# Product stage of a long convolution: sums by 64-row matmuls in two turns, another order of units, the weight additions earlier

## The chip, the cores and the metric

The kernel runs on one core of one Trainium2 chip. A core has a matmul engine (TensorE; the profile's PE, with PEld for its weight loads), VectorE (DVE), ScalarE (ACT), GpSimd (POOL), and SyncE (SP), which here only issues DMAs. They run side by side and wait for each other through semaphores. Matmuls write to PSUM, a memory of eight banks of 512 float32 per partition; all else lies in SBUF. The metric is device time in microseconds (us), lower is better.

## The reference

Two layers on 2048 tokens of width 512: a convolution as long as the sequence, gated by the layer-normed input, and a dense MLP with ReLU, both with a residual:

```python
def _A_ref(q, k, v, shift_k, ssm_k, ssm_D):      # q is layernorm(x)
    for t in range(ks):                          # ks = 4 taps
        k_shift = k_shift + k_pad[:, t:t + S, :] * shift_k[:, ks - 1 - t][None, None, :]
    kv = k_shift * v
    kv_f = rfft(kv padded to 2 S);  kf_f = rfft(ssm_k padded to 2 S)
    y = irfft(kv_f * kf_f)[:, :S, :]
    return q * (y + kv * ssm_D)

h = x + _A_ref(_layernorm(x), A_k, A_v, A_shift_k, A_ssm_k, A_ssm_D)
h2 = h + relu(_layernorm(h) @ w1) @ w2
```

(The transforms are shortened here: they stand in the original with their axes and reshapes.)

## The kernel before

The transforms are matmuls with sine tables, in two steps each. The kernel's stages, in order: taps and first step of the transforms (`pkv`, `ps`: lines 335 and 300), the **product stage** (lines 426 to 469), two steps back (`psi`, line 555; `pz`, line 646), and the MLP (`ps1m`, `ps2m`: lines 658 and 674). Each engine runs its instructions in the order in which the program gives them; nothing reorders them, so the loops below are the order.

When the product stage begins, `BK` holds the half-transformed convolution kernel and `BX` the half-transformed input, both 128 partitions by 2 by 32 by 64 values of kind float32r. For each of 32 indices `k1` the stage must finish the transform of both and multiply them. It does this in **units**. A unit takes a pair of PSUM banks (`bank2`, four such pairs in the pool `psF`) and fills it in two halves: columns 0 to 255 of both banks from `BK` (K half), columns 256 to 511 from `BX` (X half).

- `pairs(k1)`, tile `u`: the two halves of the partitions apart. For each of K and X, two steps `i` accumulate, and in each step two matmuls of 64 rows by 128 columns, one on partitions 0 to 63, the other on 64 to 127, go to the first and to the second bank. The weights are columns of the sine table `st`. There are 32 such units.
- `sums(k1)`, tile `us`: two indices `k1` and `k1 + 1` at once, one bank each, by matmuls of 128 rows by 128 columns, two accumulating steps each for K and X. The weights are `smc`, sums and differences of the sine table that POOL makes a chunk at a time (`sum_tables`, line 383), three chunks ahead, in three buffers. There are 16 such units.

`times(unit)` ends a unit: ScalarE copies its K half to SBUF (`ktu` or `kts`, two buffers each, line 423), and VectorE multiplies the X half in PSUM with that copy (line 450). The product of a `u` unit overwrites column `k1` of `BK`, that of a `us` unit two columns at the front of `BX`; after it, the bank pair is free for a later unit.

Eight chunks `c` of four indices each run in turn (line 454), each with the units u0 to u3 (`pairs(4c)` to `pairs(4c + 3)`), s0 and s1 (`sums(4c)`, `sums(4c + 2)`). TensorE's order in a chunk is u0, u1, s0, s1, u2, u3, each unit's K half and then its X half; in the first chunk the K halves of u0, u1, s0, s1 come ahead of their X halves. The products are taken in the order u0, u1, s0, s1, u2, u3.

POOL also adds up the four row blocks of the weight `w1` (`add_chunks`, line 416, three steps) into parts of `st` that are no longer wanted; TensorE makes column means of it right behind the stage (`column_means`, line 478, tile `pm`). In the program these steps stand behind the chunks 4, 5 and 6. `w1` itself is loaded on SP's queue at the start of the stage (line 408); the next load on that queue, of `x` (line 493), is issued when the stage is over.

Of the kernel before, what the change touches and what calls it, by code (L numbers as in the profile page):

```python
# [15 lines left out]
P = 128  # L16
# [40 lines left out]
def kernel(  # L57
# [13 lines left out]
    nc = tc.nc  # L71
# [9 lines left out]
    halves = (lo, hi)  # L81
# [15 lines left out]
    BK = bkp.tile([P, 2, 32, 32, DC * 2], F32R, tag="K", name="BK")  # L97
# [52 lines left out]
    def bank2(name):  # L150
        return psum.tile([P, 2, 512], F32, tag="ps", name=name)[:]
# [65 lines left out]
    st = stp.tile([P, 32, 192], F32R, name="st")  # L217
# [157 lines left out]
    smc = skp.tile([P, 3, 2, 4, P], F32R, name="smc")  # L375
# [3 lines left out]
    def sum_tables(c):  # L379
        ks = slice(4 * c, 4 * c + 4)  # L380
        for dp, pq in enumerate(halves):
            for i, op in ((0, ALU.subtract), (1, ALU.add)):
                nc.gpsimd.tensor_tensor(out=smc[pq, c % 3, i, :, 64 * dp:64 * dp + 64], in0=st[pq, ks, 64:128].bitcast(F32),  # L383
                                        in1=st[pq, ks, 0:64].bitcast(F32), op=op)
# [12 lines left out]
    BX = BXt[:, :, 2:66, :].rearrange("p g (i k) x -> p i g k x", i=2)  # L397
# [16 lines left out]
    def add_chunks(step):  # L414
        o, a, b = ((wsum, w1[:, 0, :], w1[:, 1, :]), (wpair, w1[:, 2, :], w1[:, 3, :]), (wsum, wsum.bitcast(F32), wpair.bitcast(F32)))[step]
        nc.gpsimd.tensor_tensor(out=o, in0=a, in1=b, op=ALU.add)

    def cols(B, pq, k1, i):
        return B[pq, i].rearrange("p (u w) (v s) x -> p u w v (s x)", w=2, s=2)[:, :, k1 % 2, k1 // 2, :]

    def forms(ps, tag):
        kt = prod.tile([P, 2, 256], F32, tag=tag, name=tag, bufs=2)
        nc.scalar.copy(out=kt[:], in_=ps)  # L423
        return kt

    def pairs(k1):

        ps = bank2("u")

        def do(x):  # L430
            for i, t in ((0, st[:, k1, 64:192]), (1, st[:, k1, 0:128])):
                for dp, pq in enumerate(halves):
                    nc.tensor.matmul(out=ps[:, dp, 256 * x:256 * x + 256], lhsT=t[pq], rhs=cols((BK, BX)[x], pq, k1, i),  # L433
                                     start=(i == 0), stop=(i == 1), tile_position=(64 * dp, 0), skip_group_check=True)
        return do, ps, "ktu", BK[:, :, :, k1, :]

    def sums(k1):
        ps = bank2("us")

        def do(x):  # L440
            for k in (k1, k1 + 1):
                for i in range(2):
                    nc.tensor.matmul(out=ps[:, k % 2, 256 * x:256 * x + 256], lhsT=smc[:, k // 4 % 3, i, k % 4, :],  # L443
                                     rhs=cols((BK, BX)[x], slice(0, P), k, i), start=(i == 0), stop=(i == 1), skip_group_check=True)
        return do, ps, "kts", BXs[:, :, k1:k1 + 2, :].rearrange("p g k x -> p k g x")

    def times(unit):
        do, ps, tag, o = unit
        kt = forms(ps[:, :, 0:256], tag)
        nc.vector.tensor_tensor(out=o, in0=ps[:, :, 256:512].rearrange("p b (g x) -> p b g x", x=8),  # L450
                                in1=kt[:].rearrange("p b (g x) -> p b g x", x=8), op=ALU.mult)


    for c in range(8):
        units = [pairs(4 * c), pairs(4 * c + 1), sums(4 * c), sums(4 * c + 2)]

        for n, x in sorted(((n, x) for n in range(4) for x in range(2)), key=lambda nx: nx[::-1] if c == 0 else nx):
            units[n][0](x)
        for k1 in (4 * c + 2, 4 * c + 3):
            times(units.pop(0))  # L460
            units.append(pairs(k1))
            for x in range(2):
                units[-1][0](x)
        for unit in units:
            times(unit)
        if c + 3 < 8:
            sum_tables(c + 3)
        if c in (4, 5, 6):
            add_chunks(c - 4)

    FS = 344
    cen = {}
# [25 lines left out]
    st = late.tile([P, 4, 6], F32, name="st")  # L498
# [260 lines left out]
```

## Time and profile before

| | |
|---|---|
| median of 3 runs | 208.73 us (208.56 to 209.94) |
| the profiled execution's own time | 208.83 us |
| its span on the core | 206.4 us |
| busy: TensorE, VectorE, ScalarE, POOL | 96%, 69%, 57%, 34% |
| product stage in that execution | 49.55 (first matmul of a unit) to 87.42 (end of the last product) |
| 64-row matmuls of `u`: 256 of them | 0.28 us each, two at a time |
| 128-row matmuls of `us`: 128 of them | 0.28 us each |
| copies on ScalarE: 48 | 0.59 us each |
| products on VectorE: 48 | 0.68 us each |
| granted TensorE clock over the span | 0.994 of full speed |

The span is the time from the first to the last instruction of the core; the execution's own time has 2.4 us more around it. Matmuls follow each other before the one ahead has ended, so a matmul's duration is longer than its share of the engine; the starts tell what one costs. In the timeline, a row merges equal instructions that follow each other: start, time from the first's start to the last's end, engine, line, operation, output and inputs, shapes, how many; then in brackets how long the engine had been idle ahead of it and which work ended that.

### The profile page before, as it was taken

The page shows a single profiled execution, that of the slowest core. Times are in us where ns is not written, and L with a number is a line of the kernel's source. Part 1 is how long each engine was busy: PE and PEld are TensorE (multiplying, and loading weights), DVE is VectorE, ACT ScalarE, POOL GpSimd, SP SyncE. Part 2 cuts the span into 40 slices and gives each one's busy share as a digit, 9 for nine tenths or more (in the row PEclk, how much of TensorE's full clock was granted, in tenths as well). Part 3 has the DMA queues.
Part 4 walks back from the last instruction along what each step waited for, and adds up shares of the span by engine and source line. Part 5 has one row for each costly group of instructions (what it writes and reads, how often), then busy time and mean ns, then how long its engine had stood idle before and what let it go on. Part 6 is the DMA issues. An engine that isn't in the chain of part 4 may idle for free.

```text
span 206.4 us, 4344 instructions
## 1 busy us (share of the span) xinstructions
PE 198.7 (96%) x1733; PEld 138.3 (67%) x1741; DVE 141.8 (69%) x246; ACT 117.3 (57%) x190; POOL 69.5 (34%) x118
## 2 busy tenths in 40 slices
PE   8999999998999999999999999999999999999991
PEld 2575556877899998899998944466444844444450
DVE  5989898698689989997743775899079742261131
ACT  5776789787687787777692068403950065026300
POOL 7963801991555699232003032042202010002000
PEclk9999999999999999999999999999999999999997
DMA  5999990001600000035515999999906717110011
GB/s 147 353 205 168 203 162 6 0 5 21 258 0 0 3 0 3 0 105 102 96 35 180 229 224 121 212 145 134 114 17 118 161 25 91 42 56 17 0 51 51
DMA packets 47818, 19.91 MB, mean 96 GB/s; under 512 B 42710, under 2 KB 46264, under 8 KB 47800
## 3 DMA queue, kind: packets, MB, share of 16 engines
q1 hardware_dynamic: 44144, 16.15, 42.4%
q10 hardware_dynamic: 3656, 3.51, 6.0%
q8 instruction: 13, 0.21, 0.4%
q14 instruction: 5, 0.04, 0.1%
HBM read 7.02 MB, written 2.10 MB: 44 GB/s over the span
## 4 chain that ended last, share of the span: by engine, by line
PE 94%; DVE 2%; ACT 1%; issue 1%; ACTq 0%
PE ps1m L658 18%; PE ps2m L674 18%; PE psi L555 11%; PE u L433 8%; PE us L443 8%; PE ps L300 8%; PE pz L646 7%; PE pkv L335 7%; PE psz L156 4%; PE pst L284 4%; DVE BK L450 1%; ACT ktu L423 1%; ACT BX L273 0%; DVE BK L312 0%; ACT BK L315 0%
## 5 line engine op out<-in xcount | busy, mean ns | idle before, releaser
L660 ACT ACTIVATE M<-ps1m 128x512 bf16<-128x512 f32 (+1 forms) x44 | 25.1, 595 | 49.4 <-PE ps1m L658 28.1
L674 PE MATMUL ps2m<-M 128*128 128x512 bf16 (+3 forms) x183 | 38.5, 366 | 0.2
L674 PEld LDWEIGHTS <-M 128*128 128x128 bf16 (+1 forms) x187 | 18.3, 98 | 19.9
L658 PEld LDWEIGHTS <-w 128*128 128x128 bf16 (+1 forms) x176 | 17.4, 100 | 19.9
L383 POOL TENSOR_TENSOR smc<-st 64x256 fp32r<-64x256 f32 x32 | 22.8, 731 | 13.6 <-PE us L443 12.8
L517 POOL TENSOR_SCALAR rstd<-mv 128x4 f32<-128x4 f32 x8 | 2.2, 277 | 70.1 <-DVE mv L515 70.1
L676 DVE SCALAR_TENSOR_TENSOR M<-ps2m,rstd,M 128x512 bf16<-128x512 f32 (+1 forms) x13 | 9.1, 705 | 22.6 <-PE ps2m L674 13.5
L450 DVE TENSOR_TENSOR BK<-u,ktu 128x512 fp32r<-128x512 f32 x32 | 20.6, 685 | 4.9 <-PE us L443 2.7
L555 PE MATMUL psi<-inv,BK 128*128 128x128 f32 x128 | 21.1, 255 | 0.0
L423 ACT COPY ktu<-u 128x512 f32<-128x512 f32 x32 | 18.0, 588 | 5.1 <-DVE BK L450 2.4
L555 PE MATMUL psi<-inv,BX 128*128 128x256 f32 x64 | 20.5, 338 | 0.1
L555 PEld LDWEIGHTS psi<-inv,BK 128*128 128x128 f32 x128 | 19.7, 197 | 0.0
L658 PE MATMUL ps1m<-M,w 128*128 128x512 bf16 (+1 forms) x88 | 19.3, 379 | 0.0
L658 PE MATMUL ps1m<-xT,w 128*128 128x512 bf16 (+1 forms) x88 | 19.3, 379 | 0.0
L433 PE MATMUL u<-BK,st 64*128 64x256 f32 x128 | 14.2, 303 | 0.0
L433 PE MATMUL u<-BX,st 64*128 64x256 f32 x128 | 13.0, 283 | 0.0
L555 PEld LDWEIGHTS psi<-inv,BX 128*128 128x128 f32 x64 | 12.1, 196 | 0.4 <-DVE BK L450 0.4
L513 DVE BATCH_NORM_STATS2 st<-M 128x6 f32<-128x512 bf16 x20 | 12.3, 677 | 0.0
L315 ACT CAST BK<-ps 128x512 fp32r<-128x512 f32 x16 | 9.3, 585 | 5.0 <-PE ps L300 3.4
L632 DVE TENSOR_TENSOR qT<-pz,qT 128x2048 bf16<-128x2048 f32 x2 | 4.6, 2291 | 10.7 <-DMA qT<-M 6.5
L443 PE MATMUL us<-BK,smc 128*128 128x256 f32 x64 | 10.8, 294 | 0.7 <-ACT BX L273 0.6
L450 DVE TENSOR_TENSOR BX<-us,kts 128x512 fp32r<-128x512 f32 x16 | 10.9, 685 | 0.8
(126 smaller groups left out, 405.5 us busy)
## 6 DMA issues: line engine op xcount, KB each, us to landing
E<-in_A_ssm_k_dram SPq DMA_DIRECT2D x1, 2048.0 KB
out_dram<-M ACTq DMA_DIRECT2D x15, 128.0 KB
w<-in_B_w_dram SPq DMA_DIRECT2D x1, 1376.0 KB
M<-in_B_w_dram ACTq DMA_DIRECT2D x1, 1280.0 KB
M<-in_A_q_dram SPq DMA_DIRECT2D x8, 128.0 KB
xh<-in_A_q_dram SPq DMA_DIRECT2D x4, 128.0 KB
xr<-in_A_q_dram SPq DMA_DIRECT2D x4, 128.0 KB
out_dram<-M ACTq DMA_DIRECT2D x2, 64.0 KB
```

What stands on the lines that cost most here:

```text
L300: nc.tensor.matmul(out=pss[rp][:, gi // 2, :, gi % 2, :], lhsT=fl[rows, 2 * g:2 * g + 2, :].rearrange("p d n -> p (d n)"), rhs=f[rows].rea ...
L335: nc.tensor.matmul(out=ps[:, i, :], lhsT=wdiag[:, r0 + i, j, :], rhs=kT[c][:, r0 + i, 16 - j:CH + 16 - j], start=(j == 0), stop=(j == KS - 1))
L383: nc.gpsimd.tensor_tensor(out=smc[pq, c % 3, i, :, 64 * dp:64 * dp + 64], in0=st[pq, ks, 64:128].bitcast(F32), in1=st[pq, ks, 0:64].bitcas ...
L423: nc.scalar.copy(out=kt[:], in_=ps)
L433: nc.tensor.matmul(out=ps[:, dp, 256 * x:256 * x + 256], lhsT=t[pq], rhs=cols((BK, BX)[x], pq, k1, i), start=(i == 0), stop=(i == 1), tile ...
L443: nc.tensor.matmul(out=ps[:, k % 2, 256 * x:256 * x + 256], lhsT=smc[:, k // 4 % 3, i, k % 4, :], rhs=cols((BK, BX)[x], slice(0, P), k, i) ...
L450: nc.vector.tensor_tensor(out=o, in0=ps[:, :, 256:512].rearrange("p b (g x) -> p b g x", x=8), in1=kt[:].rearrange("p b (g x) -> p b g x", ...
L555: nc.tensor.matmul(out=o if part == 0 else o[:, P * part - P:P * part], lhsT=src[:, g // 2, :, g % 2::2].rearrange("p c r -> p (c r)"), rh ...
L646: nc.tensor.matmul(out=pz[:, i, :, a:a + w, :].rearrange("p (s r) a n -> p s r (a n)", s=2), lhsT=ax[rho][:, n2 // 2, n2 % 2, :], rhs=ecor ...
L658: nc.tensor.matmul(out=ps1[:fsz, :].rearrange("p (i t) -> p i t", i=4), lhsT=w1[:, c, fc * P:fc * P + fsz], rhs=hT[sc][:, :, c, :], start= ...
L660: nc.scalar.activation(out=h1T[:fsz, fc, :], in_=ps1[:fsz, :], func=ACT.Relu)
L674: nc.tensor.matmul(out=ps2, lhsT=h1T[:ksz, fc, i * P:(i + 1) * P], rhs=w2[:ksz, fc, d0:d0 + w], start=(fc == 0), stop=(fc == NFC - 1))
```

## The change

The sums become matmuls of 64 rows too. A 128-row matmul of index `k` is now two matmuls, of partitions 0 to 63 and of 64 to 127, that add into the same bank. Each K or X half of a unit of sums is done in two **ways**: in way 1 the lower rows work on the first index (first bank) while the upper rows work on the second (second bank); in way 2 they are swapped. A no-operation of TensorE stands where the way changes and waits for the last matmuls of the other way, so that the two row halves never write to one bank at the same time. Only the first matmuls of a unit have the flag that starts a sum; all others add or, on columns not yet written, write.

The order of the units is written out as two strings, one for the first chunk and one for the others. `s0K1` is the K half of s0 in way 1, `u1X` the X half of u1, `=s0` the product of s0. The units of sums now alternate with the others, in three to five stretches each, and so the order of the products changes as well: u1, s0, u0, s1, u2, u3 in the first chunk, then u0, s0, u1, s1, u3, u2.

The three additions for `w1` move to behind the chunks 2, 4 and 5.

```diff
     def sums(k1):
+
         ps = bank2("us")
-
-        def do(x):
-            for k in (k1, k1 + 1):
-                for i in range(2):
-                    nc.tensor.matmul(out=ps[:, k % 2, 256 * x:256 * x + 256], lhsT=smc[:, k // 4 % 3, i, k % 4, :],
-                                     rhs=cols((BK, BX)[x], slice(0, P), k, i), start=(i == 0), stop=(i == 1), skip_group_check=True)
+        begun = []
+        ways = {}
+
+        def do(what):
+            x, way = "KX".index(what[0]), int(what[1])
+            last = {}
+            for i in range(2):
+                for dp, pq in enumerate(halves):
+                    k = k1 + (dp + way - 1) % 2
+                    if i == 0 and dp == 0 and (3 - way, dp) in ways:
+
+                        turn = nc.tensor.nop()
+                        for d in range(2):
+                            tc.add_manual_dep(turn.ins, ways[3 - way, d], mybir.DependencyInfo(mybir.DependencyClass.Sync, mybir.DependencyReason.DATA))
+                    mm = nc.tensor.matmul(out=ps[:, k % 2, 256 * x:256 * x + 256], lhsT=smc[pq, k // 4 % 3, i, k % 4, :],
+                                     rhs=cols((BK, BX)[x], pq, k, i), start=not begun, stop=(i == 1 and what in begun),
+                                     tile_position=(64 * dp, 0), skip_group_check=True)
+                    last[dp] = mm.ins.name
+                begun.extend((what[0] + "12"[2 - way], i))
+            for dp in range(2):
+                ways[way, dp] = last[dp]
         return do, ps, "kts", BXs[:, :, k1:k1 + 2, :].rearrange("p g k x -> p k g x")
...
+    FIRST = "s0K2 u1K s1K2 s0K1 u0K s1K1 s0X1 u1X =u1 s0X2 =s0 s1X1 u0X =u0 s1X2 =s1 u2K u2X u3K =u2 u3X =u3"
+    OTHER = "s0K1 s0X1 u0K u0X s0K2 u1K =u0 s0X2 =s0 s1K1 s1X1 u1X =u1 s1K2 s1X2 =s1 u3K u2K u3X =u3 u2X =u2"
     for c in range(8):
-        units = [pairs(4 * c), pairs(4 * c + 1), sums(4 * c), sums(4 * c + 2)]
-
-        for n, x in sorted(((n, x) for n in range(4) for x in range(2)), key=lambda nx: nx[::-1] if c == 0 else nx):
-            units[n][0](x)
-        for k1 in (4 * c + 2, 4 * c + 3):
-            times(units.pop(0))
-            units.append(pairs(k1))
-            for x in range(2):
-                units[-1][0](x)
-        for unit in units:
-            times(unit)
+        units = {}
+        for step in (OTHER if c else FIRST).split():
+            if step[0] == "=":
+                times(units[step[1:]])
+                continue
+            u = step[:2]
+            if u not in units:
+                units[u] = (pairs if u[0] == "u" else sums)(4 * c + (1 if u[0] == "u" else 2) * int(u[1]))
+            units[u][0](step[2:])
         if c + 3 < 8:
             sum_tables(c + 3)
-        if c in (4, 5, 6):
-            add_chunks(c - 4)
+        if c in (2, 4, 5):
+            add_chunks(max(c - 3, 0))
```

In `pairs` only the start flag changes in the same manner, and the halves are named K and X.

More of the change, by code (lines that the diff above doesn't have):

```diff
@@ L428, in pairs @@
         ps = bank2("u")
-        def do(x):
-            for i, t in ((0, st[:, k1, 64:192]), (1, st[:, k1, 0:128])):
+        begun = []
+        def do(what):
+            x = "KX".index(what[0])
+            for i in range(2):
+                t = st[:, k1, 64:192] if i == 0 else st[:, k1, 0:128]
                 for dp, pq in enumerate(halves):
                     nc.tensor.matmul(out=ps[:, dp, 256 * x:256 * x + 256], lhsT=t[pq], rhs=cols((BK, BX)[x], pq, k1, i),
-                                     start=(i == 0), stop=(i == 1), tile_position=(64 * dp, 0), skip_group_check=True)
+                                     start=not begun, stop=(i == 1), tile_position=(64 * dp, 0), skip_group_check=True)
+                begun.append(i)
         return do, ps, "ktu", BK[:, :, :, k1, :]
@@ L438, in sums, with do @@
         ps = bank2("us")
-        def do(x):
-            for k in (k1, k1 + 1):
-                for i in range(2):
-                    nc.tensor.matmul(out=ps[:, k % 2, 256 * x:256 * x + 256], lhsT=smc[:, k // 4 % 3, i, k % 4, :],
-                                     rhs=cols((BK, BX)[x], slice(0, P), k, i), start=(i == 0), stop=(i == 1), skip_group_check=True)
+        begun = []
+        ways = {}
+        def do(what):
+            x, way = "KX".index(what[0]), int(what[1])
+            last = {}
+            for i in range(2):
+                for dp, pq in enumerate(halves):
[11 more added lines that the diff above has]
+                ways[way, dp] = last[dp]
         return do, ps, "kts", BXs[:, :, k1:k1 + 2, :].rearrange("p g k x -> p k g x")
```

## The prediction

> **What bounds the kernel now.** I read the page first (engine shares, the chain), then the timeline of the product stage (49.6 to 87.4 us), the only stage that the change touches, and last the groups of its lines.
>
> ```profile
> PE 198.7 (96%) x1733; PEld 138.3 (67%) x1741; DVE 141.8 (69%) x246; ACT 117.3 (57%) x190; POOL 69.5 (34%) x118
> PE 94%; DVE 2%; ACT 1%; issue 1%; ACTq 0%
> ```
>
> TensorE ends nearly every wait, so a change there is worth what it takes from TensorE, as long as the next bound is far. In this stage it is not far. One chunk of the steady part:
>
> ```profile
> 77.33 0.41 PE L433 MATMUL u<-BX,st 64*128 64x256 f32 x4
> 77.43 1.29 DVE L450 TENSOR_TENSOR BK<-u,ktu 128x512 fp32r<-128x512 f32 x2
> ...
> 77.58 0.43 PE L433 MATMUL u<-BK,st 64*128 64x256 f32 x4
> ...
> 77.85 0.41 PE L433 MATMUL u<-BX,st 64*128 64x256 f32 x4
> 78.21 1.18 ACT L423 COPY ktu<-u 128x512 f32<-128x512 f32 x2 [0.33 <-DVE BK L450]
> 78.24 0.55 PEld L443 LDWEIGHTS us<-BK,smc 128*128 128x128 f32 x4 [0.20 <-issue]
> 78.27 0.73 PE L443 MATMUL us<-BK,smc 128*128 128x256 f32 x4
> 78.72 0.55 PEld L443 LDWEIGHTS us<-BX,smc 128*128 128x128 f32 x4
> 78.84 0.65 PE L443 MATMUL us<-BX,smc 128*128 128x256 f32 x4
> 79.11 1.29 DVE L450 TENSOR_TENSOR BK<-u,ktu 128x512 fp32r<-128x512 f32 x2 [0.39 <-PE us L443]
> ...
> 79.32 0.64 PE L443 MATMUL us<-BK,smc 128*128 128x256 f32 x4
> ...
> 79.80 0.64 PE L443 MATMUL us<-BX,smc 128*128 128x256 f32 x4
> ...
> 80.37 0.51 PE L433 MATMUL u<-BK,st 64*128 64x256 f32 x4
> ...
> 80.72 0.42 PE L433 MATMUL u<-BX,st 64*128 64x256 f32 x4
> ...
> 82.60 0.54 PEld L443 LDWEIGHTS us<-BK,smc 128*128 128x128 f32 x4 [0.21 <-issue]
> ```
>
> From start to start a group of four 64-row matmuls (two pairs, each pair side by side) takes 0.24 us, and four 128-row matmuls take 0.48. So a pair of 64 rows costs the same 0.1215 us as one matmul of 128 rows; call this a **slot**. A chunk has 32 slots, 3.89 us, but lasts 82.60 - 78.24 = 4.36. The missing 0.47 lies at the two crossings between the forms. Into the sums: 77.85 + 0.24 = 78.09 was due, it starts at 78.27, and its first four take 0.57 for 0.48: together 0.27. Out of them: 79.80 + 0.48 = 80.28 was due, it starts at 80.37, and its first four take 0.35 for 0.24: 0.20.
>
> VectorE sits close behind: two products take 1.29 us, each 0.685, so they follow each other every 0.605, and six per chunk want 3.63 of the 4.36; its idle 0.39 waits for the sums.
>
> **What sets when a bank pair comes free.** There are four bank pairs, and a new unit gets the one that a product freed longest ago, that is, the product four back. The start of the stage shows the price of a late one: the first product runs from 53.24 to 53.93, the weight load that waited for it starts at 53.98 (0.05 later), and the first four matmuls take 0.35 instead of 0.24, since a held weight load can't be fetched a slot ahead: matmuls follow 0.105 after it. From the same stretch: matmul start to end 0.285; end of the unit to ScalarE's copy 0.04 (57.70 to 57.73); the copy 0.588; to the product 0.03; the product 0.685; to the weight load 0.053, or 0.115 where a unit of sums also checks POOL, which takes a 0.05 us instruction of its own (78.12, the first product's end, to 78.24). So from the start of a unit's last pair until its bank pair can be used again lie 0.285 + 0.04 + 0.588 + 0.03 + 0.685 + 0.053 = 1.68 us, and 0.105 more until matmuls run: fourteen to fifteen slots, when nothing queues.
>
> **The table.** I wrote the stage out by these rules, every half-unit with its earliest start. For the kernel before, it gives 4.353 us per chunk and a last product that ends at 87.39; the trace has 4.36 and 87.42. Of the 0.27 at the crossing into the sums 0.07 is a bank pair freed late. Nothing was fitted beyond the rows above.
>
> **The change, part by part.**
>
> *64-row sums.* Each 128-row matmul becomes two of 64 rows side by side: 128 more matmuls, but the same 32 slots, if these pairs run as the other units' do (same shape, a bank each). What goes is the crossing, 0.195 each way when nothing else is late, 0.39 per chunk and some 3.5 us in all with the two extra crossings in the first chunk.
>
> The Trainium skill, page "TensorE: Matmul & The Clock Gate", section "The mechanism", says that weight loads overlap running matmuls only where the row group differs. By that a second pair in the same rows could not load ahead, and splitting the sums would cost. The trace disagrees for the same shape: at 77.49 a weight load of the other units starts while matmuls of its own row groups (77.33, 0.41 long) still run, and their slots stay at 0.12. It is kept as a rival below.
>
> *The turn.* Where the tiles swap banks, the no-operation is gone in the built program and its wait sits on the next weight load; by the wait list two of four per later chunk remain (second way, K half, of each sum), four in the first. Behind it on TensorE's queue waits all of the stage. No matmul here waited for a matmul, so the price is bounded: the release takes at least nothing, and at most 0.27, the dearest hold in the stage (the crossing into the sums). I take the nearest rows, one engine's end to another's start: 0.04. For s0 five slots, 0.61 us, lie from the last pair of the first way to the first of the second, against 0.285 + 0.04 + 0.105 = 0.43: hidden under u0. For s1 only u1's X half stands between: three slots, 0.365, against 0.43: **0.065 late** per chunk. A longer wait is partly covered, for waits on banks come right behind it: in the table 0.08 in place of 0.04 moves nothing, 0.27 adds 1.3 us.
>
> *New order.* It lengthens the time for which units hold bank pairs (s0 from slot 0 to 13 of the chunk, u1 and s1 five half-units each), and VectorE gets u3 and u2 just 0.24 apart, though it needs 0.605 between. One chunk of the table: u1's last matmul ends at 71.01; copy 71.05; product 71.67 to 72.35; plus 0.115 is 72.47, matmuls at 72.57. The next chunk's s0, to which that pair goes, was due at 72.39: **0.18 late**. Then s1 (72.96) delays u0 by 0.06, u2 delays s1 by 0.09 to 0.12, u0 and s0 delay u3 and u2 by 0.02 to 0.05. With the turn, 0.42 to 0.43 per chunk.
>
> So per chunk: minus 0.195 (out of the sums), minus 0.26 (into them, its late bank included), minus 0.01 (other late banks); plus 0.42 to 0.43. **4.353 becomes 4.32**. In the first chunk three crossings go (0.6), yet both tables arrive at u2 at 54.02: it waits for the first product, which in both needs a unit's X half, after BX is evacuated at 50.98. The last product ends at 87.24 instead of 87.39.
>
> *w1's additions.* POOL has 2.82 + 2.82 + 3.16 us of them. Before they end at 83.59, 2.3 us ahead of the column means (85.89). In the new place the first stands ahead of the tables of chunks 6 and 7: these end at 71.7 and 74.6, wanted at 76.9 and 81.2. Its w1 has landed (the DMA share is 0.00 from 58.6 on), VectorE's products keep 0.68 to 0.69 beside POOL's additions. Nothing gained, nothing lost; SP's queue is not passed, and its load of x, at 87.57, moves with the end.
>
> **The sum.** -0.15 us on the profiled execution: 208.83 (206.4 of it span) becomes 208.7. That execution stands 0.10 above the median, so the median 208.73 becomes **208.6**. Wherever the end of the stage goes, all behind it (TensorE again, to the end) follows.
>
> **Rivals.**
> 1. *Banks come free in time* (0.08). If the delays of banks are overstated, TensorE runs at 3.89 + 0.065 and the last product ends at 83.2: 204.5. If VectorE then needs its full 0.685 per product, 85.5: 206.8. For: the crossings do go. Against: the same rules give the old kernel to 0.03 us.
> 2. *The turn costs more* (0.10), slower: at the waits of s0 and s1 the queue runs dry. It decides where the release takes over 0.1 us: 0.16 gives 209.1, 0.27, the upper end, 209.9; only past 0.37, which no row here reaches, does it pass 1%. For: nothing in the trace shows a matmul's wait on a matmul. Against: 0.04 to 0.055 between all other engines.
> 3. *It doesn't do what it says* (0.03): the crossing is due not to the form but to another source of weights; then it recurs at eight alternations per chunk, last product 95.7, 217. Against: from unit to unit among the others no gap shows.
> 4. *The sums' pairs don't run side by side* (0.02), as by the rule above: two slots each, last product 98.7, 220.
>
> Forecast 0.77, its own range 207.9 to 209.3 (a product every 0.59 or 0.64 moves the difference to -0.24 or +0.04, a release of 0.03 or 0.08 to -0.41 or +0.15, and repeats of the old kernel spread to 209.94). The wide range, 207.2 to 210.2, leaves out rivals 1, 3 and 4 and the far end of 2, some 0.16. One per cent, 2.1 us, is about what a measurement here tells from no change: faster 0.07 (most of 1), slower 0.08 (3, 4 and 0.03 of 2), same 0.85.
>
> **What would show it.** Right: sums at 64 by 128, four of them every 0.24; no 0.2 us gap between kinds of unit; in its place gaps ahead of s0 and s1 released by VectorE; a chunk of 4.3 us; VectorE near 84% busy; the column means still at 85.7. Wrong: a chunk under 4.1 (rival 1), TensorE idle ahead of the second way (2), or a unit of sums of 1.9 us (4).

## The result, and the profile after

| | before | after |
|---|---|---|
| median of 12 runs each, alternating on one chip | 209.04 us (208.55 to 209.94) | 208.20 us (208.03 to 208.69) |
| ratio, with its 95% interval | | 0.9965 [0.9952, 0.9977] |
| the profiled execution's own time | 208.83 us | 208.08 us |
| its span | 206.4 us | 206.3 us |
| product stage in it (first matmul of a unit to the end of the last product) | 37.87 us | 37.65 us |
| mean of the later chunks | 4.36 us | 4.33 us (4.32 to 4.34, by the row from which it is counted) |
| end of the last product | 87.42 | 87.25 |

The time fell by 0.35%, which is real (the interval leaves 1 out) and well under the 1% that the chances were drawn at: "no change", as forecast. But of the 0.75 us between the two profiled executions only some 0.1 to 0.2 lie inside the span. The rest of this document is about two questions: whether the small gain in the stage came about as the forecast says, and where the other half microsecond is from.

First the page of the kernel after: busy time, share of the span and instructions of each engine.

```profile
PE 198.5 (96%) x1861; PEld 139.0 (67%) x1869; DVE 142.5 (69%) x246; ACT 117.2 (57%) x190; POOL 69.4 (34%) x118
```

TensorE has its 128 matmuls more and is busy as long as before. In the chain of work that ended last, VectorE has 7% of the span where it had 2%, but that is not the stage: of these 14.1 us 10.4 lie ahead of it and 2.7 in it (1.4 before), and in a second profile of the same kernel (*after_again* below) VectorE has 2% again. In the stage TensorE now waits for products and not for a change of form; its matmuls in the timeline of one later chunk show it (start, time from the first start to the last end, engine, line, output and inputs, how many; line 459 is the sums, 437 the other units, 471 the products):

```profile
69.03 0.41 PE L437 MATMUL u<-BX,st 64*128 64x256 f32 x4
69.27 0.41 PE L459 MATMUL us<-BK,smc 64*128 64x256 f32 x4
69.52 0.42 PE L437 MATMUL u<-BK,st 64*128 64x256 f32 x4
69.77 0.41 PE L459 MATMUL us<-BX,smc 64*128 64x256 f32 x4
70.02 0.51 PE L459 MATMUL us<-BK,smc 64*128 64x256 f32 x4
70.37 0.41 PE L459 MATMUL us<-BX,smc 64*128 64x256 f32 x4
70.61 0.40 PE L437 MATMUL u<-BX,st 64*128 64x256 f32 x4
70.86 0.50 PE L459 MATMUL us<-BK,smc 64*128 64x256 f32 x4
71.19 0.41 PE L459 MATMUL us<-BX,smc 64*128 64x256 f32 x4
71.43 0.66 PE L437 MATMUL u<-BK,st 64*128 64x256 f32 x8
71.92 0.65 PE L437 MATMUL u<-BX,st 64*128 64x256 f32 x8
72.52 0.51 PE L459 MATMUL us<-BK,smc 64*128 64x256 f32 x4
72.84 0.44 PE L459 MATMUL us<-BX,smc 64*128 64x256 f32 x4
73.08 0.46 PE L437 MATMUL u<-BK,st 64*128 64x256 f32 x4
73.38 0.41 PE L437 MATMUL u<-BX,st 64*128 64x256 f32 x4
```

Read the starts. From 69.03 to 70.02 the kinds of unit change at every row, and each starts 0.24 to 0.25 after the one ahead: the crossings are gone. Four places take longer than 0.24: s1 at 70.02 (0.35 to the next row), the second way of s1 at 70.86 (0.33), s0 of the next chunk, which is due at 71.92 + 0.49 = 72.41 and starts at 72.52 and takes 0.32, and u0 behind it at 73.08 (0.30). They make 0.11 + 0.09 + 0.19 + 0.06 = 0.45 us in this chunk. In the mean of chunks 2 to 6 these places take 0.10, 0.09, 0.17 and 0.05, and u1 and u2 0.02 each. From the weight loads of the same chunk, and then two of its products:

```profile
69.15 0.31 PEld L459 LDWEIGHTS us<-BK,smc 64*128 64x128 f32 x4
...
70.02 0.30 PEld L459 LDWEIGHTS us<-BK,smc 64*128 64x128 f32 x4
...
70.84 0.30 PEld L459 LDWEIGHTS us<-BK,smc 64*128 64x128 f32 x4
...
72.49 0.33 PEld L459 LDWEIGHTS us<-BK,smc 64*128 64x128 f32 x4
...
73.03 0.30 PEld L437 LDWEIGHTS u<-BK,st 64*128 64x128 f32 x4
```

```profile
71.69 0.69 DVE L471 TENSOR_TENSOR BK<-u,ktu 128x512 fp32r<-128x512 f32 x1 [0.15 <-ACT ktu L423]
72.29 0.68 DVE L471 TENSOR_TENSOR BX<-us,kts 128x512 fp32r<-128x512 f32 x1
```

The one at 69.15, which waits for nothing, starts 0.12, a slot, ahead of its matmul (69.27); those at 70.02, 70.84, 72.49 and 73.03 start within 0.05 of theirs. They were held: for a bank pair at s1, s0 and u0, for the matmuls of the other way at the turn. The products show the bank pairs: u1's ends at 71.69 + 0.69 = 72.38, and s0's weight load, which needs its pair, starts 0.11 later; s1's ends at 72.29 + 0.68 = 72.97, and u0's load starts 0.06 later; u2's of the chunk ahead ends at 69.97, and s1's load starts 0.05 later.

The stage as a whole, before and then after (stretch, length, then busy time and instructions of TensorE, its weight loads, VectorE, ScalarE and POOL, the granted clock, the DMA share, GB/s):

```profile
49.55:87.42 37.87, 37.02 (x399) 33.49 (x392) 32.11 (x51) 28.22 (x49) 23.06 (x23) 1.00 0.12 39
```

```profile
49.60:87.25 37.65, 36.82 (x523) 34.24 (x520) 32.73 (x51) 28.14 (x49) 23.05 (x23) 1.00 0.12 39
```

The stage is 0.22 us shorter; VectorE is busy for 87% of it (85% before). The clock is full in both.

### The profile page after: what moved, and what is told of

It reads as the page before. It is cut to its first block, busy times and chain, and to the rows that moved or that the text cites. A ratio compares the mean times of both kernels' runs of the same rounds, so it can differ in the third digit from the quotient of the medians.

```text
span 206.3 us, 4591 instructions
## 1 busy us (share of the span) xinstructions
PE 198.5 (96%) x1861; PEld 139.0 (67%) x1869; DVE 142.5 (69%) x246; ACT 117.2 (57%) x190; POOL 69.4 (34%) x118
## 4 chain that ended last, share of the span: by engine, by line
PE 87%; DVE 7%; ACT 2%; DMA 1%; issue 1%; DVEq 0%; ACTq 0%
PE ps1m L680 19%; PE ps2m L696 18%; PE psi L577 11%; PE us L459 8%; PE ps L300 8%; PE u L437 7%; PE pz L668 7%; PE pkv L335 7%; PE pst L284 2%; DVE E L44 1%; DVE BK L471 1%; DMA wsh<-in_A_shift_k_dram 1%; DVE G L222 1%; DVE G L220 1%; ACT ktu L423 1%
## 5 line engine op out<-in xcount | busy, mean ns | idle before, releaser
L471 DVE TENSOR_TENSOR BK<-u,ktu 128x512 fp32r<-128x512 f32 x32 | 21.3, 688 | 4.6 <-ACT ktu L423 3.3
L459 PE MATMUL us<-BK,smc 64*128 64x256 f32 x128 | 15.0, 313 | 0.4 <-ACT BX L273 0.4
L459 PE MATMUL us<-BX,smc 64*128 64x256 f32 x128 | 13.2, 284 | 0.0
L437 PE MATMUL u<-BK,st 64*128 64x256 f32 x128 | 12.9, 294 | 0.3 <-DVE BK L471 0.3
L437 PE MATMUL u<-BX,st 64*128 64x256 f32 x128 | 11.9, 281 | 0.0
```

The costliest lines, as they stand in the source:

```text
L459: mm = nc.tensor.matmul(out=ps[:, k % 2, 256 * x:256 * x + 256], lhsT=smc[pq, k // 4 % 3, i, k % 4, :], rhs=cols((BK, BX)[x], pq, k, i), s ...
```

## Experiments

All ratios are against the kernel before, in alternating runs on the same chip. "Stage" is measured as in the table above.

### 1. The change again, and its smallest part alone

*after_again* is the changed kernel once more, beside the experiments that follow; *e1_additions_alone* is the kernel before with w1's additions in their new places:

```diff
-        if c in (4, 5, 6):
-            add_chunks(c - 4)
+        if c in (2, 4, 5):
+            add_chunks(max(c - 3, 0))
```

> The changed kernel once more, beside its predecessor on one chip. Theory (the table of the stage): the stage ends 0.15 us earlier and the span is 0.1 to 0.2 shorter, so any gain in the median beyond 0.2 lies outside the span (the time less the span, 2.4 us in the profiled execution before, 1.8 after). Rival: a gain of about 0.7 shows inside the span too, and the first pair of profiled executions was a slow one against an ordinary one.

> The kernel before with w1's additions behind chunks 2, 4 and 5, nothing else. Theory: hidden on POOL at both places; 0.0 us (within 0.2), last product at 87.4, chunk 4.36. Rival: the gain beyond the stage comes from here (POOL done earlier, less beside VectorE): 0.5 us faster.

Measured: after_again 208.20 us, ratio 0.9965 [0.9944, 0.9987], stage 37.66. The additions alone 208.99, ratio 0.9997 [0.9976, 1.0018], stage 37.86 against 37.87. The gain is there again, with a median span of 206.3 us against 206.5 of the kernel before beside it, so most of it lies outside the span. The additions have no part in it that these runs can tell.

### 2. The turn with nothing in front of it

The changed kernel's 64-row sums in the old order of units, so that the two ways of a sum's half stand side by side and the second must wait for the first:

```diff
-    FIRST = "s0K2 u1K s1K2 s0K1 u0K s1K1 s0X1 u1X =u1 s0X2 =s0 s1X1 u0X =u0 s1X2 =s1 u2K u2X u3K =u2 u3X =u3"
-    OTHER = "s0K1 s0X1 u0K u0X s0K2 u1K =u0 s0X2 =s0 s1K1 s1X1 u1X =u1 s1K2 s1X2 =s1 u3K u2K u3X =u3 u2X =u2"
+    FIRST = "u0K u1K s0K1 s0K2 s1K1 s1K2 u0X u1X s0X1 s0X2 s1X1 s1X2 =u0 u2K u2X =u1 u3K u3X =s0 =s1 =u2 =u3"
+    OTHER = "u0K u0X u1K u1X s0K1 s0X1 s0K2 s0X2 s1K1 s1X1 s1K2 s1X2 =u0 u2K u2X =u1 u3K u3X =s0 =s1 =u2 =u3"
```

> The 64-row sums with their turns in the old order of units, so that in each sum the second way's K half follows the first way's X half with nothing between. Theory (a turn is released 0.04 us after the last matmul's end and its weight load runs 0.105 ahead of the matmuls, so an uncovered turn is 0.31 late, two per later chunk): chunk 4.89, 4.2 us slower than the kernel before, some 213.1. If the wait empties the queue (0.27 instead of 0.04): 8.4 slower, 217. If a matmul's wait on a matmul is free (no more than the slot): 0.4 slower, 209.3.

Measured: 213.53 us, ratio 1.0209 [1.0152, 1.0266], stage 42.71 (4.84 more than before), a chunk 4.98. One turn in it, first the weight load that waits (in brackets the idle time ahead and what ended it), then the matmuls:

```profile
69.28 0.30 PEld L459 LDWEIGHTS us<-BK,smc 64*128 64x128 f32 x4 [0.27 <-PE us L459]
```

```profile
68.81 0.40 PE L459 MATMUL us<-BX,smc 64*128 64x256 f32 x4
69.28 0.51 PE L459 MATMUL us<-BK,smc 64*128 64x256 f32 x4
69.63 0.41 PE L459 MATMUL us<-BX,smc 64*128 64x256 f32 x4
```

The last matmul of way 1 ends at 68.81 + 0.40 = 69.21; the weight load that waits for it starts at 69.28, 0.067 us after it by the unrounded times. Over the 18 turns of this run it is 0.056 to 0.075 us (0.04 was assumed in the forecast), by the profile's ends of matmuls, which are modelled. From 68.81 to 69.63 stand two groups of four that take 0.48 when nothing waits and 0.82 here: an uncovered turn costs 0.33 us, against 0.31 by the rules of the forecast. So the 64-row sums without the order that covers their turns make the kernel 2% slower. Of the 1.09 us by which a chunk is longer here than its 32 slots, some 0.68 are the two turns; the rest, 0.41, stands at units whose bank pair comes late. The order of units is what the change lives on. With 0.065 in the table the stage comes out 4.7 us longer, with 0.04 4.2.

### 3. The crossing by itself

The new alternation of units with the old 128-row sums, so that the form changes four times per chunk instead of twice:

```diff
-            x, way = "KX".index(what[0]), int(what[1])
...
+            x = "KX".index(what[0])
+            for k in (k1, k1 + 1):
+                for i in range(2):
+                    nc.tensor.matmul(out=ps[:, k % 2, 256 * x:256 * x + 256], lhsT=smc[:, k // 4 % 3, i, k % 4, :],
+                                     rhs=cols((BK, BX)[x], slice(0, P), k, i), start=(i == 0), stop=(i == 1), skip_group_check=True)
...
+    FIRST = "s0K u1K s1K u0K s0X u1X =u1 =s0 s1X u0X =u0 =s1 u2K u2X u3K =u2 u3X =u3"
+    OTHER = "s0K s0X u0K u0X u1K =u0 =s0 s1K s1X u1X =u1 =s1 u3K u2K u3X =u3 u2X =u2"
```

> The 128-row sums (no turns) in an order near the new one: each sum in one piece, the kinds alternating, so four crossings between the forms per chunk instead of two. Theory (a crossing costs 0.195 by itself): chunk 5.2, 6.7 us slower than the kernel before, some 215.6. If a crossing cost nothing by itself and only the banks freed late did: 2.5 slower, 211.5; at half the price, 4.0 slower.

Measured: 215.22 us, ratio 1.029 [1.0233, 1.0347], stage 44.54 (6.67 more than before), a chunk 5.24. In its timeline (line 450 is the sums here, 437 the other units):

```profile
68.23 0.41 PE L437 MATMUL u<-BK,st 64*128 64x256 f32 x4
68.56 0.75 PE L450 MATMUL us<-BK,smc 128*128 128x256 f32 x4
69.15 0.65 PE L450 MATMUL us<-BX,smc 128*128 128x256 f32 x4
69.73 0.51 PE L437 MATMUL u<-BX,st 64*128 64x256 f32 x4
70.07 0.84 PE L437 MATMUL u<-BK,st 64*128 64x256 f32 x8
```

Into the sums: due at 68.23 + 0.24 = 68.47, started at 68.56, and 0.59 to the next row instead of 0.48: 0.20. Out of them: due at 69.15 + 0.48 = 69.63, started at 69.73, and 0.34 instead of 0.24: 0.20. The price belongs to the change between 64 and 128 rows, and each further crossing costs it again. In a chunk the four of them are 0.78; the rest of it, 5.24 - 3.89 - 0.78 = 0.57, is put down to bank pairs that come late: in chunk 5, s0's matmuls start 0.15 and u2's 0.05 after the end of the product that frees their pair. By the table it was 5.23, and a stage 6.7 us longer. In the kernel after, the same alternation in one form shows no such gap (rows 69.03 to 70.02 above).

### 4. Bank pairs that come free sooner

If the late bank pairs are what is left of the gain, an order that frees them sooner must bring it. In *e4_u3_before_u2* both halves of u3 stand ahead of u2's, so that VectorE gets u3 a stretch earlier and can start on u2 when it is done; *e5_first_chunk_too* (run again as *e5_again*) also gives the first chunk an order in which the first product comes sooner. Of the two changed lines the first is e5's alone, the second is in both:

```diff
-    FIRST = "s0K2 u1K s1K2 s0K1 u0K s1K1 s0X1 u1X =u1 s0X2 =s0 s1X1 u0X =u0 s1X2 =s1 u2K u2X u3K =u2 u3X =u3"
-    OTHER = "s0K1 s0X1 u0K u0X s0K2 u1K =u0 s0X2 =s0 s1K1 s1X1 u1X =u1 s1K2 s1X2 =s1 u3K u2K u3X =u3 u2X =u2"
+    FIRST = "u0K s0K2 s0K1 u1K u1X s0X1 =u1 s1K1 s0X2 s1X1 u0X s1X2 s1K2 u2X =s0 u2K =u0 =s1 u3K u3X =u2 =u3"
+    OTHER = "s0K1 s0X1 u0K u0X s0K2 u1K =u0 s0X2 =s0 s1K1 s1X1 u1X =u1 s1K2 s1X2 =s1 u3K u3X u2K =u3 u2X =u2"
```

> The changed kernel with one exchange in the later chunks: u3's X half ahead of u2's K half (u3K u3X u2K, then u3's product), so that the two products at a chunk's end are not ready 0.24 us apart. Theory (banks freed late hold TensorE): chunk 4.22 instead of 4.33, stage 0.84 shorter than the changed kernel's. If TensorE's own turns or its slots held the stage, the exchange changes nothing in it (0.0). Outside the span: this program has 313 instructions on VectorE, the kernel before 314 (2.1 to 2.4 around its span), the changed one 306 (1.8); if that number decides, the 2.1 comes back and the median falls by 0.5 alone, to 207.7; if not, to 207.4.

> As e4, and the first chunk in another order: u0 and both K ways of s0 first, while the other banks are still read out of the stage before, and the first product after u1's X half, with no work of s1 ahead of it. Theory: chunk 4.22, first product at 52.2 instead of 53.2, stage 1.6 shorter than the changed kernel's; median 206.6, or 206.9 if the time around the span is 2.1. If the start was held by BX alone, 0.8 shorter as e4.

> The version with both new orders once more, for comparison on the same chip: span 204.9, around it 2.12, median 207.0.

Measured: e4 207.76 us, ratio 0.9949 [0.9931, 0.9967], stage 36.80, a chunk 4.222 (by the table 4.22). e5 207.02, ratio 0.9906 [0.9887, 0.9925], stage 36.10; on another chip 206.88, ratio 0.9907 [0.9891, 0.9924]. Against the kernel after the stage is 0.85 shorter (table 0.84) and 1.55 shorter (table 1.62). The same places of a later chunk in e4:

```profile
69.78 0.42 PE L459 MATMUL us<-BX,smc 64*128 64x256 f32 x4
70.02 0.42 PE L459 MATMUL us<-BK,smc 64*128 64x256 f32 x4
70.26 0.43 PE L459 MATMUL us<-BX,smc 64*128 64x256 f32 x4
```

s1 at 70.02 now takes its 0.24: the hold of 0.11 is gone, and nothing but the place of u3's X half was changed. What a chunk still has over its slots, 0.33, stands at s0, at u0 and at the turn of s1. In the first chunk the first product starts in the kernel after, and then in e5, at:

```profile
53.19 0.69 DVE L471 TENSOR_TENSOR BK<-u,ktu 128x512 fp32r<-128x512 f32 x1 [2.25 <-ACT ktu L423]
```

```profile
52.45 0.69 DVE L471 TENSOR_TENSOR BK<-u,ktu 128x512 fp32r<-128x512 f32 x1 [1.28 <-ACT ktu L423]
```

With it the first bank pair comes free 0.75 earlier and the other five of the first chunk 0.57; the expectation had the first product at 52.2, a whole microsecond earlier, and the stage shorter by 1.6. So the wait for bank pairs is shown as what holds the stage: where it is shortened, the stage shortens by what the table says, to 0.1.

One thing in e4 doesn't fit the stage: it is 0.85 us shorter there than the kernel after, but its median is only 0.44 lower. That leads to the next experiments.

### 5. The time around the span

An execution's time is longer than its span. Over all runs of this study the difference is 2.19 us in the kernel before (median of 58 runs, none under 2.10) and 1.80 in the kernel after (24 runs, 21 of them under 2.10). These 0.4 us are more than the stage gave. What differs outside the span? POOL, ScalarE and the DMAs have the same work in both. TensorE has 128 matmuls more. VectorE has the same 246 counted instructions, but fewer waits of their own among them, since the new order makes the products wait less often. The rows for the products' line, before and then after (duration, first and last start):

```profile
L450 DVEq EVENT_SEMAPHORE  x18: 21/21/21, 49.8 to 85.8; - x18
```

```profile
L471 DVEq EVENT_SEMAPHORE  x10: 21/21/21, 49.7 to 82.9; - x10
```

Eight instructions fewer, 314 become 306 in VectorE's program (the traces record two less of each). So *e6_eight_more_vector* puts eight back into the kernel after, late in the program at a place where VectorE is idle (they write a small constant that is no longer used):

```diff
+    for _ in range(8):
+        nc.vector.memset(n2c[:], 0.0)
```

> The changed kernel with eight more instructions on VectorE (memsets of one column that nobody reads any more), behind the last gate, where VectorE waits for TensorE. The span stays (206.3 to 206.4). If the length of VectorE's program decides the time around the span, it grows from 1.8 to 2.1 and the median to 208.5; if not, 208.2.

Measured: 208.78 us, ratio 0.9993 [0.998, 1.0006], whose interval lies above that of the kernel after, [0.9952, 0.9977], and just overlaps that of after_again, [0.9944, 0.9987]. Stage 37.69 and the span's median 206.5 are within 0.2 us of the kernel after; around the span lie 2.25 us instead of 1.80. Eight instructions of VectorE that run while it has nothing to do take the whole gain away, and in none of these 12 runs is the time around the span under 2.12.

The other way round, instructions were taken from VectorE: *e8_before_norms_on_pool* moves eight normalizations of the kernel before to POOL, *e7_norms_on_pool* does so in e5.

```diff
-            nc.vector.tensor_scalar(out=src[:, i, :], in0=src[:, i, :], scalar1=mv1[:, t, 0:1],
+            (nc.gpsimd if q > 1 else nc.vector).tensor_scalar(out=src[:, i, :], in0=src[:, i, :], scalar1=mv1[:, t, 0:1],
```

> The kernel before, its product stage untouched, with the eight norms of the last two token quarters moved from VectorE to POOL, where gates wait for neither: VectorE's program is 306 instructions instead of 314, POOL's longer. Theory (the length of VectorE's program sets the time around the span): span 206.4 to 206.6 as before, around it 1.8 instead of 2.15, median 208.3. Rival (the order of units does it): around it stays at 2.15, median 208.8.

> The version with both new orders, and the same eight norms on POOL: 306 instead of 313 instructions on VectorE. Theory: span 204.8 to 204.9 as without, around it 1.8 instead of 2.12, median 206.6 to 206.7. Rival: 207.0, or later if the norms on POOL delay a gate.

Measured: e8 215.77 us, ratio 1.0325 [1.0305, 1.0346]; e7 214.0, ratio 1.0226 [1.0199, 1.0253]. Both missed: the span grew by some 7 us. The reason is a price that no row of the kernel before had shown. In e7, on POOL, and in the kernel before, on VectorE (shortest, median and longest in ns):

```profile
L557 POOL TENSOR_SCALAR M<-M,mv,rstd x8: 2070/2076/2080, 136.4 to 170.2; 128x512 bf16<-128x512 bf16 x8
```

```profile
L535 DVE TENSOR_SCALAR M<-M,mv,rstd x8: 395/408/703, 138.3 to 160.1; 128x512 bf16<-128x512 bf16 x8
```

Four in a row are 8.3 us on POOL, and TensorE waits for them at the second layer: in e7 it stands idle for 4.7 us up to 149.33, and from 150 to 155 us its granted clock is 0.51 instead of 1.00. Half speed over 5 us is some 2.5 us more, an estimate, and the two together make the 7. What the two were made for they show in part: around the span lie 1.8 us in e7 (e5: 2.1), and 2.0 in e8 (before: 2.2), where VectorE still has 307 instructions.

The last one keeps e5's stage and takes eight instructions from VectorE where POOL has time for them: two constants, four small ones of the tables at the start, and `center` takes two instructions, each for two column blocks, instead of four.

```diff
-    nc.vector.memset(nbias[:], -0.5 * TURN)
-    nc.vector.memset(pbias[:], 0.5 * TURN)
+    nc.gpsimd.memset(nbias[:], -0.5 * TURN)
+    nc.gpsimd.memset(pbias[:], 0.5 * TURN)
...
-        nc.vector.tensor_scalar(out=t[:], in0=rows4[:], scalar1=rof[:], scalar2=v, op0=ALU.is_equal, op1=ALU.mult)
+        nc.gpsimd.tensor_scalar(out=t[:], in0=rows4[:], scalar1=rof[:], scalar2=v, op0=ALU.is_equal, op1=ALU.mult)
...
-            for n in range(4):
+            for n in range(2):
```

> The version with both new orders and eight instructions fewer on VectorE by other means: six small ones of the start on POOL, w1 centred in two instructions instead of four. VectorE's program is 305 instructions instead of 313. Theory: span 204.8 to 205.0, around it 1.8 instead of 2.12, median 206.7. Rival: around it stays at 2.1, median 207.0.

Measured: 206.44 us, ratio 0.9891 [0.9877, 0.9906], beside e5's 206.88, 0.9907, on the same chip. Its four runs have 1.74, 2.03, 2.00 and 1.75 around the span (e5 there: median 2.11), and the span's median is 0.2 shorter. It is the fastest of this study, 1.1% under the kernel before.

Side by side, with the instructions of VectorE's program (its waits included) and the weight loads of TensorE; e2 and e3 have two runs, e7, e8 and e9 four or five, the others six or more:

| kernel | VectorE | weight loads | around the span, median |
|---|---|---|---|
| before | 314 | 1741 | 2.19 us |
| e1 | 314 | 1741 | 2.36 |
| e2 | 314 | 1869 | 2.17 |
| e6 | 314 | 1869 | 2.25 |
| e4 | 313 | 1869 | 2.22 |
| e5 | 313 | 1869 | 2.12 |
| e8 | 307 | 1741 | 2.0 |
| after | 306 | 1869 | 1.80 |
| e3 | 306 | 1741 | 1.81 |
| e7 | 306 | 1869 | 1.82 |
| e9 | 305 | 1869 | 1.9 |

Neither TensorE's program (e3 against after, e6 against after) nor the length of the span (e3's is 7 us longer than after's) sorts these rows. VectorE's program does, if not to the instruction: e8 and e9 lie between the two groups. That eight instructions more move the time outside the span by 0.4 us is shown by e6 against after; that eight fewer take it back is shown in part by e9, whose four runs stand at 1.75 and at 2.0.

Why is not shown. A late fetch of instructions by DMA does not explain it. The profiled executions of e1, e4, e5 and e6 have a fetch that starts 1.7 to 2.3 us after the last instruction, and each of these executions has 2.5 to 3.2 us around its span, more than the median of its kernel. Before, e2, e8 and e5_again, which is the kernel of e5, have no such fetch and 1.9 to 2.4 us; e7 has one, 0.6 us after the last instruction, and 1.8 us. So the late fetch goes with single long executions and not with the step between 1.8 and 2.1.

## Why the prediction was right, and where it was not

**What bounds the stage: right.** Slots of 0.1215 us, VectorE close behind, and bank pairs that can be used 1.68 us after a unit's last pair gave the chunk of the kernel after as 4.32 us (measured 4.33) and the end of the last product as 87.24 (87.25). The same rules gave e3's chunk to 0.01 and the gains of e4 and e5 to 0.01 and 0.07.

**64-row sums: right.** Their pairs run side by side, four in 0.24, and the crossing, 0.195 each way, is due to the change of form (experiment 3). So rivals 3 and 4 are out. By the sentence of the Trainium skill that the forecast weighed (page "TensorE: Matmul & The Clock Gate", section "The mechanism": weight loads overlap running matmuls only where the row group differs) such a group would have taken 0.48, by the two slots for a pair that the forecast's rival 4 estimates; the trace has 0.24.

**The turn: the size of its release was off.** It was taken as 0.04 and measured as 0.056 to 0.075 (experiment 2). s0's turn is hidden, as said. At s1's, 0.09 us are lost, where 0.065 was said. By the forecast a release of 0.08 in place of 0.04 moves nothing in the sum, since waits on banks come right behind it; rival 2 needed more than 0.1.

**New order: right.** Of the late places the forecast named, in the chunk shown and in the mean of chunks 2 to 6: s0 is late by 0.19 and 0.17 (said 0.18), s1 by 0.11 and 0.10 (0.09 to 0.12), u0 by 0.06 and 0.05 (0.06); u2 only in the mean, by 0.02, and u3 not at all (0.02 to 0.05 for both). With the turn this eats 0.45 of the 0.47 that the crossings had cost, and rival 1, with banks in time, is out. Experiment 4 shows that the stage shortens where this wait does. VectorE's share of the stage came out at 87% (85% before), where "near 84%" was said from six products at 0.605 in a chunk; a product that ends in a wait counts with its full 0.685.

**w1's additions: right**, by experiment 1: ratio 0.9997. The last of them starts at 77.67 in the kernel after and takes 3.17, so it ends at 80.84, 4.7 us ahead of the column means.

**The sum: its term for the stage was right, a term was missing.** It said -0.15 us; the stage gave -0.22, and its end came 0.17 sooner. What failed is the step from there to the time, "Wherever the end of the stage goes, all behind it (TensorE again, to the end) follows": it holds for the span, whose median went from 206.5 to 206.3, but takes the 2.4 us around the span as a constant. They shrank by 0.4 (2.19 to 1.80, medians), nearly twice what the stage gave, because the new order needs eight waits fewer on VectorE. Together 0.6 of the 0.73 us that the ratio stands for; its interval, 0.48 to 1.0, holds the rest. So the forecast of 208.6 was 0.4 high against 208.20. Of the gain it had the stage's part and its mechanism. The larger part came from outside the span, for a reason that the forecast didn't have; that its range, drawn for other terms, still holds the time is luck.

## What to carry to other kernels

Where VectorE needs nearly as long per chunk as TensorE (3.63 and 3.89 us here), write the stage out slot by slot, with the time at which each PSUM bank pair comes free: removing a stall of TensorE (here 0.47 us per chunk) is worth only what the waits for bank pairs leave of it (0.03), and an exchange of two steps in the order (e4) gave the stage four times what the change gave. Put independent work of at least the latency between a matmul and one that waits for it; uncovered, the turn cost 0.33 us each time here. Before a gain of a few tenths of a microsecond is put down to a stage, compare the spans and not only the times: here two thirds of it lay outside.

## What was not expected of the hardware

- The time around the span is no constant of the kernel: medians of 1.8 to 1.9 us with 305 to 306 instructions in VectorE's program, 2.0 with 307, 2.1 to 2.4 with 313 to 314, and eight memsets in an idle stretch move it (1.80 to 2.25). The cause is open.
- A normalization of 128x512 in bf16 with two scalars per partition takes 2.07 us on POOL and 0.41 on VectorE. The Trainium skill, page "GPSIMD Engine Reference", section "4.1 Engine selection", calls elementwise work with one input "roughly line-rate" on POOL; here it is five times as long as on VectorE.
- A matmul's weight load that waits for matmuls of its own engine starts 0.056 to 0.075 us after the last of them ends (e2, 18 turns); a change between 64-row and 128-row matmuls costs some 0.2 us in each direction (e3: 0.20 and 0.20).
